# Sparse attention with a mixture of experts: where a part's third gather enters the list that orders the instructions

## The chip, the cores and the metric

The kernel runs on one core of a Trainium2 chip. The metric is the device time of one execution in microseconds (us), lower is better. Times of the kernel before are from three runs; the rows come from one more execution, taken with the profiler.

## What is computed

The input is a batch of 8 with 8 heads, 576 positions and a head width of 64. Half of the heads attend to the 32 positions behind each one, the other half to every 32nd position. The result, 4608 tokens by 512, goes through a gate that picks two of eight experts for each token, and each expert is a two-layer network of width 1024. All in float32:

```python
def _attn_ref(q, k, v):
    scores = np.matmul(q, k.transpose(0, 1, 3, 2)) / np.sqrt(D)
    mask_local = (rel >= 0) & (rel < 32)                      # heads 0 to 3
    mask_strided = (rel >= 0) & (pos[None, :] % 32 == pos[:, None] % 32)
    attn = softmax(np.where(masks, scores, -1e9))
    return np.matmul(attn, v)

def _moe_ref(x, w_gate, w_noise, noise, w1, w2):              # x: 4608 x 512
    noisy = x @ w_gate + np.log1p(np.exp(x @ w_noise)) * noise
    top2, top2_w = the two best experts of a token and their softmax weights
    for e in range(8):
        for k in range(2):
            mask = top2[:, k] == e
            out[mask] += top2_w[mask, k, None] * (np.maximum(x[mask] @ w1[e], 0.0) @ w2[e])
```

## The kernel before

**Two kinds of work in one stream.** The attention runs batch by batch and writes its rows to x_dram in the chip's memory. After the last unit of a batch a routing step (route) computes the gate, and its twelve indirect scatters on POOL (line 824, each behind a small memset on line 823) put an entry for each token and choice into the table tab, one list per expert: token number, weight, row of x. The expert work reads these lists. Parts of the first three experts' lists are fixed ahead of time so that their work can begin while the attention of later batches is still running; TensorE then has attention and expert work in turn, and the expert work fills what the attention leaves.

**A part (a job).** The lists are cut into parts of two or three blocks; a block is 128 rows, and a last one in a list can be a tail of 64. Each part goes through these steps:
- gather (line 908): SP loads the part's entries, POOL computes indices (lines 947, 950, 967, 969) and gathers the rows of x, block by block, into the tile xg. xg is a ring two deep: the third block takes the place of the first. An early part (one whose rows are known before the last batch, whole in the code) gathers a block with one indirect DMA (line 973 of the kernel before). A late part gathers a block with four of them, each of 128 rows of 128 columns, and a tail with two (line 959).
- transposes (line 981): each block is transposed, by TensorE into a bank of PSUM in an early part (line 998) and by DVE into the tile xr, one deep, in a late part (line 1002). ACT copies it rounded into xhi (line 1009) and DVE puts what the rounding left into xlo (line 1011). xhi and xlo are one deep, so a part's blocks can't be written before layer 1 of the part ahead is done with them.
- layer1 (line 1023): twelve matmuls for each of eight slices (line 1037), then ACT (line 1056) and DVE (line 1061).
- previous (line 1072): POOL gathers what the output holds so far for a block's tokens into prev (line 1077), a ring four deep.
- layer2 (line 1084): 24 matmuls for a whole block (line 1099), DVE multiplies by the weight and adds into prev (line 1124), and POOL scatters prev to the output (line 1129).

The loop over the parts makes, for part n in this order: two prev gathers of n, the gather step of n + 1, layer 1 of n, the transposes of n + 1, layer 2 of n. There are 32 parts counting the early ones; 16 of them have three blocks: two of the seven early parts, and 14 of the late ones, 8 of these with a tail as the third block.

**What sets the order.** Nothing above issues an instruction at once. Each step is a Piece (line 230) with an engine, a cost, a rank and the pieces that it waits for. issue_all (line 291) then runs a list schedule over all pieces with its own clock: on each engine it takes, among the pieces that could begin within 120 ns of the earliest, the one of lowest rank. A gather has the rank of its part's place (100 per part, plus 1), a prev gather plus 0 or 4, an output scatter plus 4 or more. The order that comes out is the order of each engine's queue on the chip. The chip's own waits are put in later, from what each instruction reads and writes, and an engine takes its queue in order: an instruction that waits holds up all behind it. On POOL that is every table scatter, every gather, every prev gather and every output scatter.

What a piece waits for in the list is fixed when it is made. For a place in a ring it is this, in the constructor:

```python
for s in self.alloc:
    r = s.ring
    if len(r.hist) >= r.k:
        self.deps += r.hist[-r.k].users
```

The users of a slot are the pieces that had named it by then. In the kernel before the gather step makes the gathers of all of a part's blocks before the transposes step makes the pieces that read them.

Of the kernel before, what the change touches and what calls it, by code (L numbers as in the profile page):

```python
# [22 lines left out]
def kernel(  # L23
# [12 lines left out]
    nc = tc.nc  # L36
# [43 lines left out]
    x_dram = dpool.tile([4 * NTOK, 128], F32, name="x_dram")  # L80
# [196 lines left out]
    def dma(fn, nbytes, rank, eng="SP", **kw):  # L277
        return Piece(eng, 690 if eng == "SP" else GAP, fn, rank, lat=nbytes, **kw)
# [137 lines left out]
    R = {}  # L416
# [485 lines left out]
    def experts(zero):  # L902
        W = {}
        known_stores = {n: [x for b in range(n) for x in stores[b]] for n in range(1, B + 1)}
        known_tab = {n: [x for b in range(n) for x in scatters[b]] for n in range(1, B + 1)}
        G_, XH, HT = {}, {}, {}

        def gather(n, rank):
            e, (start, nb, tail, hb) = jobs[n]
            known = hb * S  # L910

            whole = hb < B
            tb, gi = R["tabt"].new(), R["gix"].new()
            tx, gx = (None, None) if whole else (R["tabx"].new(), R["gxx"].new())

            def entries(dst, p0, n, how, bytes_, dims):
                def load(o):
                    ld = nc.sync.dma_start(dst(), dram(tab, (e * REG + p0) * 3, dims))
                    if hb < B:
                        for x, b in all_scatters:  # L920
                            if b >= hb:
                                tc.declare_no_dep(ld.ins, x.ins, reason=BEHIND)
                            else:
                                tc.add_manual_dep(ld.ins, x.ins.name, mybir.DependencyInfo(
                                    mybir.DependencyClass.Sync, mybir.DependencyReason.DATA), reason="entries of the list")
                        early_loads.append((ld, hb))
                dma(load, bytes_, rank if hb == B else 20 * NP * (hb - 1) + 10 * NP, after=known_tab[hb], expert=True,
                    far=4000, **how)

            if not whole:  # L930
                entries(lambda: tx.t[:, :4 * nb, :].rearrange("p b c -> p (b c)"), start, 128 * nb, {"alloc": [tx]}, 16384,
                        [[0, 4], [12 * nb, 32], [1, 12 * nb]])
            ng = tail // 32
            if tail:
                tx2 = R["tabx"].new()
                for g in range(ng):
                    entries(lambda g=g: tx2.t[:, g, :], start + 128 * nb + 32 * g, 32,
                            {"write" if g else "alloc": [tx2]}, 4096, [[0, 4], [3, 32], [1, 3]])
            entries(lambda: tb.t[:, :nb, :].rearrange("p b c -> p (b c)"), start, 128 * nb, {"alloc": [tb]}, 8192,
                    [[3 * nb, 4], [12 * nb, 32], [1, 3 * nb]])  # L940
            if tail:
                entries(lambda: tb.t[:tail, nb, :], start + 128 * nb, tail, {"write": [tb]}, 4096,
                        [[3, tail], [1, 3]])
            rows_known = 4 * known - 4

            def xindices(o):
                nc.gpsimd.tensor_scalar(gx.t[:, :nb, :], tx.t[:, :4 * nb, 2].rearrange(
                    "p (g b) -> p b g", g=4), float(rows_known), qoff[:, 0:1], op0=ALU.min, op1=ALU.add)
                if tail:
                    nc.gpsimd.tensor_scalar(gx.t[:, nb, :ng], tx2.t[:, :ng, 2], float(rows_known),  # L950
                                            qoff[:, 0:1], op0=ALU.min, op1=ALU.add)
            if not whole:
                Piece("POOL", 360 if tail else 230, xindices, rank, read=[tx] + ([tx2] if tail else []), alloc=[gx],
                      expert=True)
            xs = []
            for i in () if whole else range(nb + (tail > 0)):
                xg = R["xg"].new()
                for g in range(4 if i < nb else tail // 32):
                    dma(lambda o, i=i, g=g, xg=xg: nc.gpsimd.indirect_dma_start(  # L959
                        out=xg.t[:, g, :], out_offset=None, in_=x_dram[:4 * known, :],  # L960
                        in_offset=bass.IndirectOffsetOnAxis(ap=gx.t[:, i, g:g + 1], axis=0)),
                        65536, rank, eng="POOL", read=[gx], after=known_stores[hb], expert=True,
                        **({"write": [xg]} if g else {"alloc": [xg]}))
                xs.append(xg)

            def indices(o):
                nc.gpsimd.tensor_scalar(gi.t[:, :nb], tb.t[:, :nb, 0], known - 1, None, op0=ALU.min)
                if tail:
                    nc.gpsimd.tensor_scalar(gi.t[:tail, nb:nb + 1], tb.t[:tail, nb, 0:1], known - 1, None, op0=ALU.min)
            Piece("POOL", 300 if tail else 170, indices, rank, read=[tb], alloc=[gi], expert=True)  # L970
            for i in range(nb) if whole else ():
                xg = R["xg"].new()
                dma(lambda o, i=i, xg=xg: nc.gpsimd.indirect_dma_start(  # L973
                    out=xg.t.rearrange("p g c -> p (g c)"), out_offset=None,
                    in_=x_dram.rearrange("(t q) c -> t (q c)", q=4)[:known, :],
                    in_offset=bass.IndirectOffsetOnAxis(ap=gi.t[:, i:i + 1], axis=0)),
                    262144, rank, eng="POOL", read=[gi], after=known_stores[hb], expert=True, alloc=[xg])
                xs.append(xg)
            G_[n] = (tb, gi, xs)

        def transposes(n, rank):

# [2 lines left out]
            xh, xl = R["xhi"].new(), R["xlo"].new()  # L985
            XH[n] = (xh, xl)
            for i in range(nb + (tail > 0)):
                xg = G_[n][2][i]
                rows = 128 if i < nb else tail
                ng = rows // 32  # L990
                cols = slice(128 * i, 128 * i + rows)
# [15 lines left out]
                def view(xr=xr, rows=rows):  # L1007
# [3 lines left out]
                Piece("DVE", dve(4 * rows), lambda o, view=view, cols=cols: nc.vector.tensor_tensor(  # L1011
                    xl.t[:, :, cols], view(), xh.t[:, :, cols].bitcast(F32), ALU.subtract),
                      rank, read=[xr, xh], expert=True, **{how: [xl]})

        counts = {}

# [131 lines left out]
        for n, (e, (start, nb, tail, hb)) in enumerate(jobs):  # L1148
            nb += tail > 0
            others = [x for y in range(E) if y != e for x in out_done[y]]  # L1150
            rank = ER + 100 * n
# [29 lines left out]
    for c in range(NTOK // ZC):  # L1181
        zero.append(dma(
            lambda o, c=c: nc.sync.dma_start(out[ZC * c:ZC * c + ZC, :].rearrange("(p c) (a d) -> p (c a) d", p=128, a=4),
                                             zeros[:, None, :].to_broadcast([128, 4 * ZC // 128, 128])), 786432,
# [3 lines left out]
    for u in range(NU):  # L1188
        rank = 10 * u
# [20 lines left out]
    with tc.If(longest > CAP):  # L1210
        with ExitStack() as octx:
# [4 lines left out]
            for e in range(E):  # L1216
                left = nc.values_load(over[:1, e:e + 1], engines=ENG, min_val=0, max_val=NTOK - CAP)
                with tc.If(left > 0):
                    nc.sync.dma_start(w1t, dram(w1, e * DM * FF, [[FF, 128], [128 * FF, ND], [1, FF]]))
                    nc.sync.dma_start(w2t, dram(w2, e * DM * FF, [[DM, 128], [128 * DM, NF], [1, DM]]))  # L1220
                    with tc.For_i(0, left, 128) as it:
                        tb = ow.tile([128, 3], I32, name="tb")
                        nc.sync.dma_start(tb, tab[bass.ds(it + (e * REG + CAP), 128), :])
                        gi = ow.tile([128, 1], I32, name="gi")
                        nc.vector.tensor_scalar(gi, tb[:, :1], NTOK - 1, None, op0=ALU.min)
                        gx = ow.tile([128, 4], I32, name="gx")
                        xg = ow.tile([128, 4, 128], F32, name="oxg")
                        for c in range(4):
# [3 lines left out]
                                                         in_offset=bass.IndirectOffsetOnAxis(ap=gx[:, c:c + 1], axis=0))  # L1232
# [49 lines left out]
```

## Time and profile before

| what | us |
|---|---|
| median of three runs | 1108.83 |
| lowest and highest of them | 1102.39, 1113.18 |
| the profiled execution, its own time | 1104.51 |
| its span, first to last instruction | 1102.80 |
| TensorE busy in the span | 1064.4 |
| POOL busy in the span | 553.8 |
| DVE busy in the span | 607.6 |

The profiled execution is one run, 4.3 us under the median. Its own time is 1.71 us more than its span. PE is TensorE, DVE is VectorE, ACT is ScalarE, POOL is GpSimd and SP the engine that issues plain DMAs. Matmuls overlap each other, so a matmul's own duration is longer than its share of the time; the busy times count an overlap once. The granted clock (PEclk) is the mean over a stretch of what TensorE was given: 1.00 is 2.4 GHz and 0.50 is 1.2 GHz.

### The profile page before, as it was taken

The page shows a single profiled execution, that of the slowest core. Times are in us where ns is not written, and L with a number is a line of the kernel's source. Part 1 is how long each engine was busy: PE and PEld are TensorE (multiplying, and loading weights), DVE is VectorE, ACT ScalarE, POOL GpSimd, SP SyncE. Part 2 cuts the span into 40 slices and gives each one's busy share as a digit, 9 for nine tenths or more (in the row PEclk, how much of TensorE's full clock was granted, in tenths as well). Part 3 has the DMA queues.
Part 4 walks back from the last instruction along what each step waited for, and adds up shares of the span by engine and source line. Part 5 has one row for each costly group of instructions (what it writes and reads, how often), then busy time and mean ns, then how long its engine had stood idle before and what let it go on. Part 6 is the DMA issues. An engine that isn't in the chain of part 4 may idle for free.

```text
span 1102.8 us, 23359 instructions
## 1 busy us (share of the span) xinstructions
PE 1064.4 (97%) x8645; PEld 938.3 (85%) x8645; DVE 607.6 (55%) x1606; ACT 432.8 (39%) x1131; POOL 553.8 (50%) x734
## 2 busy tenths in 40 slices
PE   8898899999799999999999999999999999999995
PEld 7677678889688989898998989898988898898994
DVE  7789976776465223655673456345534553474341
ACT  6689975677353212423341224113312331142120
POOL 1045543510763455656676555655656464657530
PEclk8999999999899999999999999999999999999998
DMA  8999998887534332455554236223622452253210
GB/s 173 230 212 230 240 237 228 218 238 199 144 103 138 91 104 77 135 148 149 156 168 141 71 101 189 79 70 106 185 81 64 121 166 76 69 158 97 72 59 23
DMA packets 169482, 152.93 MB, mean 139 GB/s; under 512 B 52651, under 2 KB 137131, under 8 KB 169348
## 3 DMA queue, kind: packets, MB, share of 16 engines
q1 hardware_dynamic: 145028, 92.30, 33.4%
q0 software_dynamic: 24320, 58.87, 17.7%
q8 instruction: 82, 1.34, 0.5%
q14 instruction: 52, 0.43, 0.1%
HBM read 112.76 MB, written 39.39 MB: 138 GB/s over the span
## 4 chain that ended last, share of the span: by engine, by line
PE 82%; DVE 5%; issue 5%; DMA 4%; ACT 3%; POOL 0%; POOLq 0%; DVEq 0%; SPq 0%
PE bankE L1099 5%; PE bankF L1099 5%; PE bankG L1099 5%; PE bankC L1099 5%; PE bankG L1037 5%; PE bankF L1037 5%; PE bankA L1099 5%; PE bankH L1037 5%; PE bankC L1037 5%; PE bankA L1037 5%; PE bankD L1099 4%; PE bankB L1037 4%; PE bankD L1037 4%; PE bankE L1037 4%; PE bankH L1099 4%
## 5 line engine op out<-in xcount | busy, mean ns | idle before, releaser
L959 POOL DMA_INDIRECT xg<-x_dram,gxx x240 | 241.4, 1006 | 105.1 <-issue 55.7
L1129 POOL DMA_INDIRECT out_dram<-prev,tabt x80 | 82.1, 1026 | 103.7 <-DVE prev L1124 45.9
L1077 POOL DMA_INDIRECT prev<-out_dram,gix x80 | 77.3, 966 | 92.1 <-issue 39.5
L824 POOL DMA_INDIRECT tab<-ent,addr x96 | 92.2, 960 | 57.9 <-issue 15.6
L1002 DVE STREAM_TRANSPOSE xr<-xg 128x512 f32<-128x512 f32 (+1 forms) x64 | 66.3, 1037 | 12.7 <-DMA xg<-x_dram,gxx 11.2
L1009 ACT CAST xhi<-xr 128x512 fp32r<-128x512 f32 (+1 forms) x64 | 37.8, 591 | 69.9 <-DVE xr L1002 69.9
L894 ACT CAST w2hi<-wraw 128x512 fp32r<-128x512 f32 x80 | 47.4, 619 | 29.2 <-PE bankA L1108 7.4
L895 DVE TENSOR_TENSOR w1lo<-wraw,w1hi 128x512 fp32r<-128x512 f32 x80 | 54.7, 686 | 3.5 <-ACT w1hi L894 1.0
L895 DVE TENSOR_TENSOR w2lo<-wraw,w2hi 128x512 fp32r<-128x512 f32 x80 | 52.7, 684 | 3.5 <-ACT w2hi L894 2.2
L1011 DVE TENSOR_TENSOR xlo<-xr,xhi 128x512 fp32r<-128x512 f32 (+1 forms) x64 | 42.1, 658 | 18.4 <-ACT xhi L1009 17.2
L894 ACT CAST w1hi<-wraw 128x512 fp32r<-128x512 f32 x80 | 49.0, 614 | 1.4 <-DMA wraw<-in_moe_w_dram 1.2
L973 POOL DMA_INDIRECT xg<-x_dram,gix x16 | 16.8, 1050 | 58.4 <-PE bankD L998 42.8
L1056 ACT ACTIVATE hhi<-bankG 128x256 fp32r<-128x256 f32 (+2 forms) x34 | 14.3, 421 | 70.9 <-PE bankG L1037 70.9
L1037 PE MATMUL bankG<-xhi,w1hi 128*128 128x256 f32 (+3 forms) x136 | 41.2, 303 | 0.0
L1037 PE MATMUL bankG<-xhi,w1lo 128*128 128x256 f32 (+3 forms) x136 | 40.3, 296 | 0.0
L1037 PE MATMUL bankG<-xlo,w1hi 128*128 128x256 f32 (+3 forms) x136 | 40.1, 295 | 0.0
L1037 PE MATMUL bankF<-xhi,w1hi 128*128 128x256 f32 (+3 forms) x132 | 39.9, 302 | 0.0
L1037 PE MATMUL bankH<-xhi,w1hi 128*128 128x256 f32 (+3 forms) x132 | 39.7, 301 | 0.0
L1037 PE MATMUL bankA<-xhi,w1hi 128*128 128x256 f32 (+3 forms) x132 | 39.6, 300 | 0.0
L1037 PE MATMUL bankC<-xhi,w1hi 128*128 128x256 f32 (+3 forms) x132 | 39.6, 300 | 0.0
L1037 PE MATMUL bankF<-xhi,w1lo 128*128 128x256 f32 (+3 forms) x132 | 39.4, 298 | 0.0
L1037 PE MATMUL bankF<-xlo,w1hi 128*128 128x256 f32 (+3 forms) x132 | 39.3, 298 | 0.0
(666 smaller groups left out, 3573.1 us busy)
## 6 DMA issues: line engine op xcount, KB each, us to landing
wraw<-in_moe_w_dram SPq DMA_DIRECT2D x160, 256.0 KB
out_dram<-zeros SPq DMA_DIRECT2D x12, 768.0 KB
ks<-in_k_dram SPq DMA_DIRECT2D x15, 320.0 KB
qs<-in_q_dram SPq DMA_DIRECT2D x15, 320.0 KB
vraw<-in_v_dram SPq DMA_DIRECT2D x30, 160.0 KB
raw<-in_k_dram SPq DMA_DIRECT2D x16, 288.0 KB
v_l<-in_v_dram SPq DMA_DIRECT2D x16, 288.0 KB
raw<-in_q_dram SPq DMA_DIRECT2D x16, 288.0 KB
```

What stands on the lines that cost most here:

```text
L824: st = nc.gpsimd.indirect_dma_start(out=tab, out_offset=bass.IndirectOffsetOnAxis(ap=s["addr"].t[:, t, kk:kk + 1], axis=0), in_=s["ent"].t ...
L894: Piece("ACT", act(512) + 30, lambda o: nc.scalar.copy(hi.t, raw.t), rank, read=[raw], alloc=[hi], expert=True)
L895: Piece("DVE", dve(512), lambda o: nc.vector.tensor_tensor(lo.t, raw.t, hi.t.bitcast(F32), ALU.subtract), rank, read=[raw, hi], alloc=[lo] ...
L959: dma(lambda o, i=i, g=g, xg=xg: nc.gpsimd.indirect_dma_start(out=xg.t[:, g, :], out_offset=None, in_=x_dram[:4 * known, :], in_offset=bas ...
L973: dma(lambda o, i=i, xg=xg: nc.gpsimd.indirect_dma_start(out=xg.t.rearrange("p g c -> p (g c)"), out_offset=None, in_=x_dram.rearrange("(t ...
L1002: Piece("DVE", 8 * rows, lambda o, xg=xg, xr=xr, ng=ng, rows=rows: nc.vector.transpose(xr.t.rearrange("p (c x) -> p c x", c=ND)[:, :, :row ...
L1009: Piece("ACT", act(4 * rows), lambda o, view=view, cols=cols: nc.scalar.copy(xh.t[:, :, cols], view()), rank, read=[xr], expert=True, **{h ...
L1011: Piece("DVE", dve(4 * rows), lambda o, view=view, cols=cols: nc.vector.tensor_tensor(xl.t[:, :, cols], view(), xh.t[:, :, cols].bitcast(F ...
L1037: nc.tensor.matmul(ps.t[:, :width], a.t[:, 128 * d:128 * d + 128], c.t[:, d, :width], start=(m == 0), stop=(m == len(todo) - 1))
L1077: dma(lambda o: nc.gpsimd.indirect_dma_start(out=pv.t[:rows, :], out_offset=None, in_=out[:known, :], in_offset=bass.IndirectOffsetOnAxis( ...
L1099: nc.tensor.matmul(ps.t, HT[n, f][p[0]].t[:, cols], W2[n][f][p[1]].t, start=(m == 0), stop=(m == len(todo) - 1))
L1129: st = nc.gpsimd.indirect_dma_start(out=out[:known, :], out_offset=bass.IndirectOffsetOnAxis(ap=tb.t[:rows, i, 0:1], axis=0), in_=pv.t[:ro ...
```

## The change

The gather step makes only the gathers of a part's first two blocks and keeps a function, rows_of, that makes one block's gathers. The transposes step calls it for block i + 2 behind the pieces of block i. Ranks, costs, tiles and the work itself stay as they are.

```diff
--- before.py
+++ after.py
@@ -952,31 +952,33 @@
             if not whole:
                 Piece("POOL", 360 if tail else 230, xindices, rank, read=[tx] + ([tx2] if tail else []), alloc=[gx],
                       expert=True)
-            xs = []
-            for i in () if whole else range(nb + (tail > 0)):
+
+            def rows_of(i):
                 xg = R["xg"].new()
+                if whole:
+                    dma(lambda o: nc.gpsimd.indirect_dma_start(
+                        out=xg.t.rearrange("p g c -> p (g c)"), out_offset=None,
+                        in_=x_dram.rearrange("(t q) c -> t (q c)", q=4)[:known, :],
+                        in_offset=bass.IndirectOffsetOnAxis(ap=gi.t[:, i:i + 1], axis=0)),
+                        262144, rank, eng="POOL", read=[gi], after=known_stores[hb], expert=True, alloc=[xg])
+                    return xg
                 for g in range(4 if i < nb else tail // 32):
-                    dma(lambda o, i=i, g=g, xg=xg: nc.gpsimd.indirect_dma_start(
+                    dma(lambda o, g=g: nc.gpsimd.indirect_dma_start(
                         out=xg.t[:, g, :], out_offset=None, in_=x_dram[:4 * known, :],
                         in_offset=bass.IndirectOffsetOnAxis(ap=gx.t[:, i, g:g + 1], axis=0)),
                         65536, rank, eng="POOL", read=[gx], after=known_stores[hb], expert=True,
                         **({"write": [xg]} if g else {"alloc": [xg]}))
-                xs.append(xg)
+                return xg
+            xs = [] if whole else [rows_of(i) for i in range(2)]
 
             def indices(o):
                 nc.gpsimd.tensor_scalar(gi.t[:, :nb], tb.t[:, :nb, 0], known - 1, None, op0=ALU.min)
                 if tail:
                     nc.gpsimd.tensor_scalar(gi.t[:tail, nb:nb + 1], tb.t[:tail, nb, 0:1], known - 1, None, op0=ALU.min)
             Piece("POOL", 300 if tail else 170, indices, rank, read=[tb], alloc=[gi], expert=True)
-            for i in range(nb) if whole else ():
-                xg = R["xg"].new()
-                dma(lambda o, i=i, xg=xg: nc.gpsimd.indirect_dma_start(
-                    out=xg.t.rearrange("p g c -> p (g c)"), out_offset=None,
-                    in_=x_dram.rearrange("(t q) c -> t (q c)", q=4)[:known, :],
-                    in_offset=bass.IndirectOffsetOnAxis(ap=gi.t[:, i:i + 1], axis=0)),
-                    262144, rank, eng="POOL", read=[gi], after=known_stores[hb], expert=True, alloc=[xg])
-                xs.append(xg)
-            G_[n] = (tb, gi, xs)
+            if whole:
+                xs = [rows_of(i) for i in range(2)]
+            G_[n] = (tb, gi, xs, rows_of)
 
         def transposes(n, rank):
 
@@ -985,7 +987,8 @@
             xh, xl = R["xhi"].new(), R["xlo"].new()
             XH[n] = (xh, xl)
             for i in range(nb + (tail > 0)):
-                xg = G_[n][2][i]
+                xs, rows_of = G_[n][2:]
+                xg = xs[i]
                 rows = 128 if i < nb else tail
                 ng = rows // 32
                 cols = slice(128 * i, 128 * i + rows)
@@ -1011,6 +1014,9 @@
                 Piece("DVE", dve(4 * rows), lambda o, view=view, cols=cols: nc.vector.tensor_tensor(
                     xl.t[:, :, cols], view(), xh.t[:, :, cols].bitcast(F32), ALU.subtract),
                       rank, read=[xr, xh], expert=True, **{how: [xl]})
+                if i + 2 < nb + (tail > 0):
+
+                    xs.append(rows_of(i + 2))
 
         counts = {}
```

## Rows read from the trace of the kernel before

**Rows 1.** The page: the span, and each engine's busy time.
```profile
span 1102.8 us, 23359 instructions
...
PE 1064.4 (97%) x8645; PEld 938.3 (85%) x8645; DVE 607.6 (55%) x1606; ACT 432.8 (39%) x1131; POOL 553.8 (50%) x734
```

**Rows 2.** Stretches: length; busy PE, PEld, DVE, ACT, POOL; PEclk, DMA share, GB/s.
```profile
0.00:168.00 168.00, 148.09 (x2336) 119.46 (x2337) 137.29 (x554) 132.13 (x419) 62.39 (x140) 0.95 0.97 218
168.00:252.00 84.00, 83.99 (x1058) 72.84 (x1058) 59.44 (x220) 56.58 (x170) 27.06 (x46) 1.00 0.92 236
252.00:276.00 24.00, 24.00 (x345) 22.02 (x344) 16.85 (x54) 17.37 (x49) 0.00 (x0) 1.00 0.67 182
276.00:282.00 6.00, 3.71 (x27) 3.23 (x26) 3.46 (x24) 2.53 (x8) 4.50 (x9) 1.00 0.86 188
282.00:288.00 6.00, 6.00 (x43) 4.98 (x43) 2.92 (x15) 2.31 (x5) 4.90 (x11) 0.72 0.67 176
288.00:297.00 9.00, 9.00 (x105) 7.38 (x105) 4.85 (x18) 4.82 (x17) 5.60 (x9) 1.00 0.35 96
297.00:302.00 5.00, 1.32 (x31) 0.92 (x29) 1.09 (x3) 0.26 (x1) 3.68 (x4) 0.87 0.40 113
302.00:308.00 6.00, 6.00 (x69) 4.57 (x61) 2.95 (x10) 2.29 (x10) 4.87 (x14) 0.54 0.30 85
308.00:364.00 56.00, 55.75 (x419) 49.16 (x420) 33.68 (x104) 23.64 (x55) 27.24 (x47) 1.00 0.49 133
364.00:1060.00 696.00, 696.00 (x4065) 627.52 (x4064) 336.60 (x594) 187.51 (x393) 407.67 (x454) 1.00 0.38 114
1060.00:1102.80 42.80, 30.54 (x179) 26.26 (x178) 8.50 (x15) 3.33 (x9) 5.91 (x6) 0.88 0.10 32
```

**Rows 3.** Waits, 225 to 312 us: who waited for whom, total, times, longest.
```profile
POOL xg L973 <- PE bankD L998: 41.6, 1, 41.6
...
DVE prev L1124 <- DMA prev<-out_dram,gix: 6.8, 1, 6.8
...
PE bankF L550 <- DVE prev L1124: 3.7, 1, 3.7
...
PE bankC L998 <- DMA xg<-x_dram,gix: 2.3, 1, 2.3
```

**Rows 4.** POOL in order of time: start, duration, instruction, idle before it.
```profile
234.79 0.20 POOL L812 COPY ent<-wt 96x12 f32<-96x12 f32 x1 [0.80 <-DVE wt L806]
276.63 0.97 POOL L973 DMA_INDIRECT xg<-x_dram,gix  x1 [41.65 <-PE bankD L998]
...
277.91 0.93 POOL L824 DMA_INDIRECT tab<-ent,addr  x1 [0.21 <-POOL spacer L823]
...
291.33 0.91 POOL L824 DMA_INDIRECT tab<-ent,addr  x1 [0.21 <-issue]
...
293.86 1.01 POOL L1129 DMA_INDIRECT out_dram<-prev,tabt  x1 [0.30 <-DVE kT_s L286]
297.41 1.00 POOL L1077 DMA_INDIRECT prev<-out_dram,gix  x1 [2.54 <-DMA out_dram<-prev,tabt]
```

**Rows 5.** The chain that ended last, 270 to 312 us: start, duration, what.
```profile
276.63 4.71 DMA xg<-x_dram,gix
...
303.93 2.86 PE bankA L1099 x6
...
307.98 1.59 PE bankA L1099 x6
```

**Rows 6.** Waits of the whole span, POOL for the DVE transposes.
```profile
POOL xg L959 <- DVE xr L1002: 19.3, 15, 3.2
```

**Rows 7.** POOL, DVE and the chain around a late part's layer 1.
```profile
558.37 0.94 POOL L959 DMA_INDIRECT xg<-x_dram,gxx  x1 [0.30 <-DVE w1lo L895]
...
564.22 0.69 DVE L1011 TENSOR_TENSOR xlo<-xr,xhi 128x512 fp32r<-128x512 f32 x1
...
568.25 2.08 PE bankG L1037 x12
```

## The prediction

> **What bounds the kernel now.** I read the page's busy line first: TensorE is busy 1064.4 of 1102.8 us [rows 1], so the whole kernel can win at most the 38.4 us in which it stands still, plus what a low clock costs. Next I read the stages, in the table of stretches [rows 2], for where those 38.4 us lie. The reader is to see that they lie in three places. 19.9 us (168.00 - 148.09) are in the first 168 us, before the expert work is under way. 12.3 us (42.80 - 30.54) are in the tail after the last matmul. From 168 to 276 and from 364 to 1060 TensorE has no gap at all (0.01 us), and 0.25 us are left in 308 to 364. What remains are two short holes: 2.29 us in 276 to 282 and 3.68 us in 297 to 302. After each of them the granted clock is low (0.72 in 282 to 288, 0.54 in 302 to 308), where all other stretches from 168 to 1060 show 1.00.
>
> Then I read who ended those holes. The list of waits from 225 to 312 us [rows 3] names them: 2.3 us of a transpose (line 998) for a gather xg, and 3.7 us of the score matmuls (line 550) for the DVE step that adds a block into prev (line 1124); that DVE step itself had stood 6.8 us before the gather of prev. Above both stands a POOL wait of 41.6 us, of xg on line 973 for the transposes.
>
> Last I read POOL in order of time [rows 4]. At 234.79 us it copies the entries of a batch, and then it does nothing until 276.63, when the third gather of the part with three blocks goes out. Behind it, back to back, come twelve scatters into the table (277.91 to 291.33), two output scatters (to 293.86) and the prev gathers (from 297.41). So both holes have one cause. The gather was put in POOL's queue some 40 us before the transposes that free its place in the two-deep ring xg; POOL takes its queue in order, so all of that was late.
>
> **The change part by part.** *The place in the list.* A ring's third allocation waits for the users of the first, as far as they are known when it is made (the constructor of Piece). Before, all three gathers of a part are made ahead of the transposes, so the list knows of the first two gathers only and lets the third go as soon as the first has landed; the real wait is then POOL's. After, the third gather is made behind block 0's transposes, cast and subtraction, so the list itself holds it back. Up to 234.79 us nothing differs in the list's inputs, so the start (19.9 us) stays, and so does the tail.
>
> *What is moved.* Sixteen parts have three blocks: two of them early parts with one gather each (line 973). Of the fourteen late parts, counted by the code, eight end in a 64-row tail (two gathers) and six have a whole third block (four gathers). That is 2 + 16 + 24 = 42 of 256 gathers. None is added or removed, the bytes are the same, and SP's queue issues nothing for them. Each is moved back past what POOL has ready: table scatters, output scatters, prev gathers. No wait is added: the wait for the transposes is the one POOL already had.
>
> *The early part at 235 us.* What comes free is POOL from 235 to 276 (0.00 us busy in 252 to 276 [rows 2]). The queued work takes about 16.2 us from 277.6 to 293.9, and a few us more for the prev gathers [rows 4]; it fits in those 41 us, beside TensorE work which is full there. The gather itself still leaves at about 276.6 and lands 4.7 us later [rows 5], but the list now knows this and can put other TensorE work (the layer-2 matmuls of the part before, 1.6 us per six [rows 5]) ahead of the third transpose, where before TensorE stood for it. Terms:
> - the hole for xg: -2.29 us [rows 2, 3];
> - the hole for prev: -3.68 us [rows 2, 3];
> - the low clock behind them. From the granted clock it is 0.28 x 6 = 1.68 us in 282 to 288, 0.46 x 6 = 2.76 us in 302 to 308, and at most 0.2 us in 297 to 302, 4.6 together. From the instructions it is a little less: six layer-2 matmuls take 2.86 us at the low clock and 1.59 us at the full one [rows 5], a factor of 1.8 and not 2. The busy time at 1.2 GHz is 4.6/0.5 = 9.2 us, which at 1.8 costs 4.1. I take the middle, -4.3 us.
>
> That is -10.3 us. *What is given back:* with the holes gone, another wait can be next, an attention step on ACT or DVE. The nearest rows are 0.25 us of 56 in the stretch behind and 0.01 of 84 in the one before; the farthest is the start, 19.9 of 168, which in the 32 us from 276 to 308 would be 3.8 us. I take 0.3, as the neighbours have it, and keep 0 to 3.8 for the range.
>
> *The other early part and the fourteen late ones.* From 308 to 364 TensorE loses 0.25 us, and from 364 to 1060 nothing. POOL waits 19.3 us in 15 places for the DVE transposes there [rows 6], but no TensorE wait hangs on them, so their going brings nothing: 0 us. Can moving the gathers cost? In the part with 384 columns the last gather of the third block is issued at 558.37, its low half is done at 564.22 + 0.69 = 564.91, and layer 1 begins at 568.25 [rows 7]: 3.3 us to spare. A gather or scatter issue takes about 1.3 us with its gap, so two of them ahead of the third block (2.6 us) cost nothing and three (3.9 us) would cost 0.6. The gather's rank comes before output scatters', and a block's place comes free before the second block's gathers have all gone, so I take 0, with 0 to +22 us as bounds (below).
>
> *One rule against the change.* In the 84 us from 168 to 252 POOL was busy 27.06 us and DVE 59.44, and TensorE still 83.99 [rows 2]: side by side they cost TensorE nothing. The Trainium skill (SBUF — State Buffer, its part on the engines' ports and the DMA ports) says that GpSimd and VectorE share a pair of ports under an exclusive lock, whose loser stands for the whole instruction. By that rule POOL work that moves beside a busy DVE would slow DVE; the rows of 168 to 252 don't bear it out in TensorE's time, so the sum takes 0 for it, and what it would do at the worst is rival 4.
>
> *Sum.* 1104.51 us is the profiled execution (span 1102.80); less 10.0 it is 1094.5. The median of the runs shown, 1108.83, is 4.3 us above that execution, so I forecast **1099 us**, 0.9% below it. One per cent, 11 us, is about what a measurement of this kernel can tell from no change; the forecast lies just inside.
>
> **The rivals.**
> 1. *Only the first hole goes.* Prev stays late through another link: its gather also waits for the output scatters' landing, and the DVE step for its turn. Then 2.29 + 1.68 = 4 us: 1105. For it: two links lie between POOL and TensorE [rows 3]. Against it: all of them start 40 us sooner.
> 2. *The third gathers come too late in the late parts (slower).* Place: the third block's transposes ahead of layer 1. It decides once more than two POOL issues are put before the third gather, that is over 3.3 us late. Price: a hole of about 2 us and the clock behind it 1.7, as at 276 us, 3.7 each. In the six parts with four gathers that is 22 us: 1121. Against it: the room above, and POOL is busy only 407.67 of 696 us [rows 2].
> 3. *The change doesn't do what it says.* The list's clock for the transposes runs ahead of the chip's, so POOL still stands at the third gather: 1108.
> 4. *POOL's moved work holds DVE.* Some 16 us of POOL work [rows 4] move from where DVE is light (4.85 of 9 us) to where it is busy (16.85 of 24, so 7.15 us free [rows 2]). If DVE stood through all of it, it would be 16 - 7.15 = 9 us late, and the gain would shrink to 1 us: 1108. Against it: 168 to 252 us, as said.
>
> **How the numbers follow.** Forecast 0.72 (1092 to 1105 by itself: the give-back of 3.8 us, and what the runs scatter). Rival 1: 0.12; rival 2: 0.07; rival 3: 0.05; rival 4: 0.04. The range 1090 to 1110 holds the forecast, rivals 1, 3 and 4, and leaves out rival 2 and the edges. Faster by over 1% (under 1097.7) takes a bit under half of the forecast's own case, 0.35. Slower by over 1% is rival 2 in part, 0.06. Within 1% is the rest, 0.59.
>
> **What would show it.** Right: POOL without the 41.6 us wait on line 973 and busy between 235 and 276 us; table scatters of that batch done before the third gather; no TensorE wait on prev; granted clock 1.00 from 168 us to the tail; TensorE's busy time lower by about 4 us and its idle time by 6; after 364 us the same picture shifted 10 us earlier. Wrong: a TensorE wait on xg or xlo in the late stage, a new low-clock stretch, or POOL still standing at a third gather.

## The result and the profile after

| | us |
|---|---|
| kernel before, median of 15 runs (lowest, highest) | 1108.05 (1102.39, 1113.18) |
| changed kernel, median of 15 runs (lowest, highest) | 1098.10 (1095.13, 1101.51) |
| ratio, 95% interval | 0.9913, 0.9899 to 0.9927 |
| profiled execution of the changed kernel, its own time and its span | 1098.46, 1096.70 |

The changed kernel is 9.95 us (0.9%) faster, and the interval is clear of no change. The forecast was 1099 us, 0.9 us above the median that was measured.

The page of the changed kernel, the lines that answer to [rows 1]:

```profile
span 1096.7 us, 23359 instructions
...
PE 1062.7 (97%) x8645; PEld 939.4 (86%) x8645; DVE 607.4 (55%) x1605; ACT 432.4 (39%) x1132; POOL 552.5 (50%) x734
```

There are the same number of instructions and of matmuls, 1.7 us less of TensorE's busy time, and 6.1 us less of span. Where these went is read from the stretches, which answer to [rows 2] with the same columns:

```profile
0.00:168.00 168.00, 147.33 (x2278) 119.70 (x2280) 134.52 (x541) 130.38 (x413) 58.91 (x135) 0.91 0.94 212
168.00:252.00 84.00, 83.99 (x1087) 73.34 (x1088) 60.22 (x225) 54.93 (x163) 34.59 (x61) 1.00 0.89 228
252.00:276.00 24.00, 23.06 (x308) 21.18 (x307) 17.15 (x54) 17.57 (x54) 11.94 (x18) 1.00 0.88 231
276.00:282.00 6.00, 6.00 (x73) 5.15 (x72) 2.06 (x7) 3.16 (x10) 1.91 (x3) 1.00 0.95 268
282.00:288.00 6.00, 6.00 (x56) 5.01 (x55) 4.74 (x31) 3.92 (x12) 1.20 (x3) 1.00 1.09 331
...
297.00:302.00 5.00, 5.00 (x91) 3.72 (x90) 1.74 (x5) 2.04 (x10) 2.93 (x6) 1.00 0.02 1
302.00:308.00 6.00, 6.00 (x53) 5.29 (x51) 2.47 (x9) 2.48 (x8) 3.06 (x7) 1.00 0.20 53
308.00:364.00 56.00, 56.00 (x407) 50.38 (x407) 32.76 (x99) 23.41 (x54) 24.15 (x41) 1.00 0.47 129
364.00:1054.00 690.00, 690.00 (x4031) 621.73 (x4030) 335.30 (x591) 186.03 (x390) 403.59 (x448) 1.00 0.39 115
```

The reader is to see three things. TensorE has no gap from 276 to 1054 us, and the granted clock is 1.00 all through it: both holes and both falls of the clock are gone. POOL has 11.94 us of work in 252 to 276, where it had none. And 0.94 us (24.00 - 23.06) are missing in that stretch, where nothing was missing before.

The waits answer to [rows 3]. TensorE's only wait between 168 and 1090 us is the first line; POOL's waits for a place are the other two (one of the window 225 to 312, one of the whole span, which answers to [rows 6]):

```profile
PE bankE L509 <- DMA ks<-in_k_dram: 0.9, 1, 0.9
```

```profile
POOL xg L959 <- PE bankG L1001: 3.8, 1, 3.8
```

```profile
POOL xg L966 <- DVE xr L1005: 20.6, 17, 3.2
```

The 41.6 us have become 3.8. The late parts' waits for the DVE transposes (line 1005, line 1002 before) have not gone: 20.6 us in 17 places against 19.3 in 15. I come back to that. POOL in order of time, answering to [rows 4]:

```profile
238.93 0.20 POOL L812 COPY ent<-wt 96x12 f32<-96x12 f32 x1 [0.79 <-DVE wt L806]
...
243.87 0.95 POOL L824 DMA_INDIRECT tab<-ent,addr  x1 [4.73 <-issue]
...
263.14 0.91 POOL L824 DMA_INDIRECT tab<-ent,addr  x1 [0.22 <-issue]
265.19 1.01 POOL L1135 DMA_INDIRECT out_dram<-prev,tabt  x1 [1.14 <-ACT hhi L1062]
...
273.36 1.00 POOL L1083 DMA_INDIRECT prev<-out_dram,gix  x1 [5.36 <-DVE kT_l L286]
...
281.92 0.94 POOL L959 DMA_INDIRECT xg<-x_dram,gix  x1 [3.78 <-PE bankG L1001]
```

The scatters, the output scatters and the prev gathers now stand ahead of the third gather. **How much that is worth** is best read between two events that both traces have: from the third gather's issue to the first matmuls of layer 1 of its part. In the trace of before the latter is this line of the chain that ended last:

```profile
310.88 2.09 PE bankD L1037 x12
```

and in the changed kernel, with the line numbers moved by six:

```profile
305.13 2.09 PE bankA L1043 x12
```

Before, it took 310.88 - 276.63 = 34.25 us; after, 305.13 - 281.92 = 23.21 us: 11.04 us saved. The 0.94 us of the new wait for ks fall ahead of the third gather. From an event ahead of everything that the change moves, the copy of a batch's entries, to the same layer 1 it is 310.88 - 234.79 = 76.09 us before and 305.13 - 238.93 = 66.20 us after: **9.9 us saved**, the new wait included. The copy itself came 4.1 us later in this execution than before. Another execution of the same changed kernel (e11, below) has it at 235.61, only 0.8 us later, so the 4.1 us are a difference between executions and not the change's.

### The profile page after: what moved, and what is told of

Its sections match the earlier page's. It is cut to its first block, busy times and chain, and to the rows that moved or that the text cites. A ratio compares the mean times of both kernels' runs of the same rounds, so it can differ in the third digit from the quotient of the medians.

```text
span 1096.7 us, 23359 instructions
## 1 busy us (share of the span) xinstructions
PE 1062.7 (97%) x8645; PEld 939.4 (86%) x8645; DVE 607.4 (55%) x1605; ACT 432.4 (39%) x1132; POOL 552.5 (50%) x734
## 3 DMA queue, kind: packets, MB, share of 16 engines
q0 software_dynamic: 24320, 58.87, 17.6%
## 4 chain that ended last, share of the span: by engine, by line
PE 90%; DMA 3%; DVE 3%; ACT 2%; issue 1%; POOL 0%; POOLq 0%; DVEq 0%
PE bankF L1105 6%; PE bankC L1105 5%; PE bankG L1043 5%; PE bankD L1105 5%; PE bankH L1043 5%; PE bankC L1043 5%; PE bankA L1043 5%; PE bankE L1043 5%; PE bankB L1043 5%; PE bankG L1105 5%; PE bankH L1105 5%; PE bankF L1043 5%; PE bankE L1105 5%; PE bankD L1043 4%; PE bankA L1105 4%; PE bankB L1105 4%
## 5 line engine op out<-in xcount | busy, mean ns | idle before, releaser
L1062 ACT ACTIVATE hhi<-bankH 128x256 fp32r<-128x256 f32 (+2 forms) x33 | 14.0, 423 | 70.3 <-PE bankH L1043 70.3
L1043 PE MATMUL bankA<-xhi,w1lo 128*128 128x256 f32 (+3 forms) x132 | 39.2, 297 | 0.0
L1043 PE MATMUL bankC<-xhi,w1lo 128*128 128x256 f32 (+3 forms) x132 | 39.2, 297 | 0.0
```

Source lines behind the costliest of these rows:

```text
L1043: nc.tensor.matmul(ps.t[:, :width], a.t[:, 128 * d:128 * d + 128], c.t[:, d, :width], start=(m == 0), stop=(m == len(todo) - 1))
L1062: Piece("ACT", act(width) + 30, lambda o: nc.scalar.activation(hh.t[:, :width], ps.t[:, :width], AF.Relu), rank, read=[ps], alloc=[hh], ex ...
```

## The experiments

Twelve runs, in four series, each series on one chip with the kernel before run beside it. The chip of the first series was slower for every kernel (the kernel before: 1155.02 us, against 1106 to 1108 on the others), so its ratios are not compared with the others' (each ratio is to the kernel before on the same chip, with its 95% interval in brackets), and its four questions were asked again (e8, e9, e10, e12).

**Ahead of them: the order of the queues.** The lists of instructions of each engine, in the order in which the schedule puts them, tell what the edit moves. On POOL two gathers move, both of early parts: the third of part 3 (counted from 0) goes from ahead of a batch's twelve scatters to behind these, two output scatters and four prev gathers; the third of part 4 changes places with one index computation. With the edit in the early parts alone, the queues of all five engines are those of the changed kernel; with the edit in the late parts alone, they are those of the kernel before. So the late parts' forty gathers stay where they were, and the experiments ask which of the two moved gathers matters, and through what.

TensorE's own order changes too. In part 3 the third transposes stood 3.6 us of other work behind the first ones before (275.61 to 281.48, less the wait of 2.29); in the changed kernel (e11) they stand 9.04 us behind (276.54 to 285.58). So there are two candidates for the gain, POOL's freed queue and TensorE's new order, and e9 and e10 below have one of them each.

### One gather moved alone (e1, e8; e2, e12)

```diff
-            xs = [] if whole else [rows_of(i) for i in range(2)]
+            xs = [] if whole else [rows_of(i) for i in range(nb + (tail > 0))]
...
             if whole:
-                xs = [rows_of(i) for i in range(2)]
+                xs = [rows_of(i) for i in range(2 if n == 3 else nb)]
...
-                if i + 2 < nb + (tail > 0):
+                if i + 2 < nb + (tail > 0) and i + 2 >= len(xs):
```

This is the changed kernel with the deferral in part 3 only (late parts as before); with `n == 4` it is part 4 only.

> Only the third gather of the first early part with three blocks enters the list behind its transposes; the other early part and all late parts are as in the kernel before. Theory (the whole gain is the one POOL wait of 41.6 us at 235 us): ratio 0.991, as for the whole change, no TensorE wait on prev, granted clock 1.00 from 168 us to the tail. Rival (the late parts, where POOL waited 19.3 us for the DVE transposes, carry the gain): 1.000. Rival (the other early part has a share): 0.993 to 0.996.

> The deferral of early part 3 alone, the other parts as before. My theory (this one gather holds POOL's queue, and with it the scatters and the gathers of prev behind it): the whole gain, a ratio of 0.990 to 0.992, POOL's longest wait for a place gone, no fall of the clock between 282 and 308 us. Rival (both moved gathers are needed, half the gain each): 0.995 to 0.996.

> Only the third gather of the second early part with three blocks enters the list behind its transposes. Theory: ratio 1.000 within 0.2%, both holes of the kernel before still there (2.3 and 3.7 us), the 41.6 us POOL wait too. Rival (this part has a share): 0.995 to 0.997.

> The deferral of early part 4 alone, part 3 and the rest as before. My theory (that gather changes places with one index computation only and no table scatter stands behind it): 0.999 to 1.001, POOL's longest wait for a place still near 41.6 us and TensorE's two waits as before, 2.3 and 3.7 us. Rival (both moved gathers bring half the gain each): 0.995 to 0.996.

Part 3 alone (e8) takes 1099.04 us, a ratio of 0.9916 [0.9887, 0.9945]; on the first chip (e1) it is 0.9831 [0.9797, 0.9865]. Part 4 alone (e12) takes 1106.24 us, 1.0010 [0.9992, 1.0027]; on the first chip 0.9997 [0.9972, 1.0022]. With part 3 alone (e8) POOL's longest wait for the third gather and TensorE's only wait between 168 and 1040 us are these:

```profile
POOL xg L959 <- PE bankG L1001: 4.5, 1, 4.5
```

```profile
PE bankE L509 <- DMA ks<-in_k_dram: 0.4, 1, 0.4
```

The waits from 225 to 312 us with part 4 alone (e12) are those of before, with the second hole 1.6 us longer:

```profile
POOL xg L959 <- PE bankD L1001: 41.7, 1, 41.7
...
PE bankF L550 <- DVE prev L1130: 5.3, 1, 5.3
...
PE bankC L1001 <- DMA xg<-x_dram,gix: 2.3, 1, 2.3
```

The clock tells why it is longer. Behind the first hole, 2.30 us long as before, it didn't fall in this execution:

```profile
282.00:288.00 6.00, 6.00 (x79) 4.94 (x78) 4.66 (x16) 3.06 (x8) 4.91 (x11) 1.00 0.53 126
```

In the kernel before it was 0.72 in the same stretch [rows 2], which cost 1.68 us; here those were not lost, TensorE came to the second wait that much sooner, and waited 5.32 us in place of 3.68. From the third gather to layer 1 it still took 308.90 - 274.32 = 34.58 us. So the low clock behind the first hole came in one of two executions in which TensorE's order was the same up to there, and the one without it won nothing by that.

One of 256 gathers carries the whole gain, as far as the intervals tell (the whole change in the same series as e8, e11: 0.9897 [0.9874, 0.9921]). The one with twelve scatters, two output scatters and four prev gathers queued behind it counts; the one that changes places with an index computation doesn't.

### The order as before, the place no longer waited for (e3, e9)

```diff
-                xg = R["xg"].new()
+                xg = R["xg" if i < 2 else "xr"].new()
...
-                    out=xg.t.rearrange("p g c -> p (g c)"), out_offset=None,
+                    out=xg.t.rearrange("p g c -> p (g c)") if i < 2 else xg.t, out_offset=None,
...
```

This is the kernel before, with an early part's third block gathered into the tile xr, which only late parts use, and transposed from there. The gather stays ahead of the batch's scatters in POOL's queue, and there is no place that it waits for.

> The kernel before, but the third block of the two early parts goes into the tile xr, which stands empty until the late parts, so its gather needs no place that the transposes free. It stays where it was in the list, with the first two. Theory (what cost was POOL standing): ratio 0.990 to 0.992, third gather at about 235 us, no hole from 276 to 308 us. Rival (the gain is the list's better knowledge, which puts other TensorE work ahead of the third transposes): 0.995 or above, for the list knows no more here than before.

> The order of before, with a place of its own for the third block of an early part, so that no gather waits for a place. My theory (the wait for the place costs, not the order of the list): 0.990 to 0.992. Rival (the order of the gathers on POOL, which stays as before here, is what costs): 0.998 to 1.002.

E9 takes 1097.61 us, 0.9908 [0.9884, 0.9932]; on the first chip 0.9840 [0.9793, 0.9887]. POOL in order of time (e9):

```profile
234.94 1.05 POOL L973 DMA_INDIRECT xg<-x_dram,gix  x1 [1.03 <-DMA x_dram<-xo]
236.50 0.94 POOL L973 DMA_INDIRECT xr<-x_dram,gix  x1 [0.50 <-DVE nz L753]
```

and the third transposes on TensorE:

```profile
283.91 0.68 PE L999 MATMUL bankH<-ident,xr 128*128 128x128 f32 x4
```

The third gather leaves at 236.50 with the first two of its part, ahead of the twelve scatters as in the kernel before, and the gain is the same. So it does no harm by itself that it stands ahead of them; that it waits there does. TensorE's new order isn't needed for the gain either: the third transposes stand 3.4 us behind the first ones (at 280.49), as in the kernel before.

### The two holes, closed one at a time (e4, e10; e5)

The first edit closes the first hole and leaves POOL as it was: the schedule is told that the third transposes come 6 us behind the first ones, so that TensorE has other work ahead of them.

```diff
-                    Piece("PE", 108 * ND, tr, rank, read=[xg], psum=xr, expert=True)
+                    behind = [first] if i == 2 else []
+                    turn_it = Piece("PE", 108 * ND, tr, rank, read=[xg], after=behind, psum=xr, expert=True)
+                    if i == 0:
+                        first = turn_it
+                    if behind:
+                        turn_it.lag = 6000
```

In the schedule's clock a piece then begins its lag later than the pieces that it waits for.

> The kernel before, but the list lets the early parts' third transposes begin only 6 us behind the first ones, so TensorE does other work while the third gather lands; POOL's queue at 235 us stays as before, with its 41 us wait. Additive theory (my prediction's first rival: the first hole and its low clock go, the second stays): gain 2.3 + 1.7 = 4 us, ratio 0.9964, second hole 3.7 us. Rival theory (the second hole's end is set by POOL's chain from the third gather on, so TensorE that comes there sooner waits longer): ratio 0.999 to 1.001, the second hole grows from 3.7 to about 7 us.

> The order of before on POOL, with TensorE's wait for the gathered block put later in TensorE's list, so that the first hole is filled and POOL's stall stays. My theory (the second hole's end is set by POOL's own chain, some 25 us behind the third gather, so that it takes over what the first gives back): 0.998 to 1.001, and the wait for prev grows from 3.7 us to 6 or 7. Rival (the holes add up, and the first one is gone): 0.996 to 0.997, with the wait for prev at 3.7 us.

E10 takes 1105.22 us, 0.9985 [0.9967, 1.0003]; on the first chip 0.9977 [0.9946, 1.0007]. The stretches, POOL's lines and TensorE's in e10:

```profile
276.00:282.00 6.00, 6.00 (x69) 4.91 (x69) 2.28 (x7) 3.14 (x7) 1.29 (x3) 1.00 1.05 295
282.00:288.00 6.00, 6.00 (x62) 5.06 (x61) 5.51 (x39) 2.64 (x9) 4.90 (x11) 1.00 0.84 191
288.00:297.00 9.00, 9.00 (x109) 7.55 (x107) 5.66 (x24) 5.53 (x17) 7.36 (x14) 1.00 0.39 84
297.00:302.00 5.00, 0.69 (x9) 0.29 (x6) 0.00 (x0) 0.26 (x1) 2.15 (x3) 0.86 0.28 105
302.00:308.00 6.00, 2.53 (x44) 2.29 (x44) 2.70 (x7) 0.28 (x2) 4.64 (x10) 0.50 0.62 171
```

```profile
280.49 0.97 POOL L974 DMA_INDIRECT xg<-x_dram,gix  x1 [41.65 <-PE bankD L999]
...
301.25 1.00 POOL L1083 DMA_INDIRECT prev<-out_dram,gix  x1 [2.54 <-DMA out_dram<-prev,tabt]
```

```profile
305.47 0.40 PE L551 MATMUL bankF<-mask_s,twin 64*64 64x288 bf16 x1 [7.79 <-DVE prev L1130]
```

The first hole and the fall of the clock behind it are gone, 2.29 + 1.68 = 4.0 us, and the second hole has grown from 3.68 to 7.79, by 4.1. Its end stands at 305.47 - 280.49 = 24.98 us behind the third gather; in the kernel before, whose score matmuls begin with the line below, it was 301.65 - 276.63 = 25.02, and in e12 299.39 - 274.32 = 25.07.

```profile
301.65 0.39 PE L550 MATMUL bankF<-mask_s,twin 64*64 64x288 bf16 x1 [3.68 <-DVE prev L1124]
```

That distance is POOL's own chain: from the third gather to the first prev gather 20.76 us of scatters and of waiting for an output scatter to land, 3.4 for the prev gather's landing, 0.8 for the DVE step. In these three traces TensorE waits for its end, however early it comes.

This edit also gives TensorE the order of the changed kernel in part 3:

```profile
288.51 0.65 PE L999 MATMUL bankE<-ident,xg 128*128 128x128 f32 x4
```

The third transposes stand 9.04 us behind the first ones (at 279.47), as in e11. With POOL's stall left in place that order wins nothing clear of noise, and in e9 POOL without its stall wins the whole gain in the old order. So it is POOL's stall that cost.

The second edit fills both holes with matmuls of zeros, to keep the clock up: nine ahead of the third transposes and eighteen ahead of the score matmuls. They are extra work, in banks that the next matmuls start anew.

```diff
         def scores(o):
+            for _ in range(18 if u == 30 else 0):
+                nc.tensor.matmul(sc[0].t.rearrange("r (a x) -> r a x", a=2), warm[:, :128],
+                                 warm[:, None, :].to_broadcast([128, 2, 256]), start=True, stop=True)
...
+                        for _ in range(9 if (n, i) == (3, 2) else 0):
+                            nc.tensor.matmul(xr.t.rearrange("r (a x) -> r a x", a=2), warm[:, :128],
+                                             warm[:, None, :].to_broadcast([128, 2, 256]), start=True, stop=True)
```

> The kernel before with extra matmuls on a tile of zeros in TensorE's queue, just ahead of the two waits: 9 of 512 columns (1.9 us) ahead of the early part's third transposes, 18 (3.9 us) ahead of the score matmuls that wait for prev. They write a bank that is overwritten right behind. Theory (the low clock comes from the idle holes, and the second hole's end is set by POOL's chain): granted clock 1.00 from 276 to 308 us, the second wait longer by what the first clock fall cost, and only the second fall's 2.7 us are won: ratio 0.9976. Additive theory: 4.3 us, 0.9961. Rival (the clock falls for another reason): clock still near 0.5 behind the holes, ratio 1.000 or slower.

E5 takes 1106.07 us, 0.9995 [0.9978, 1.0012]: the expected 0.9976 was a miss. POOL's third gather, TensorE's filling and its wait, and the stretches from 300 us:

```profile
274.43 0.97 POOL L976 DMA_INDIRECT xg<-x_dram,gix  x1 [41.65 <-PE bankD L1004]
```

```profile
293.61 4.05 PE L542 MATMUL bankH<-zeros 128*128 128x512 bf16 x18
...
299.39 0.28 PE L553 MATMUL bankF<-mask_s,twin 64*64 64x288 bf16 x1 [1.46 <-DVE prev L1130]
```

```profile
300.00:302.00 2.00, 1.43 (x22) 0.97 (x13) 1.83 (x9) 0.00 (x0) 1.51 (x7) 0.93 0.67 209
302.00:304.00 2.00, 2.00 (x6) 1.16 (x4) 0.86 (x2) 1.49 (x8) 1.78 (x3) 0.50 0.08 16
```

The first fall is not there, and TensorE comes to the second wait sooner. But the hole's end is again at 299.39 - 274.43 = 24.96 us, the eighteen matmuls were over before that and left a wait of 1.46 us, and the clock fell to 0.50 behind it all the same. That the zeros kept the clock up behind the first hole is not shown: in e12 it stayed up there without them. From the third gather to layer 1 it took 308.36 - 274.43 = 33.9 us, against 34.25 before.

### A gather that really comes too late (e6), and the changed kernel again (e7, e11)

In e6 the changed kernel's late parts hold the third block's gathers until the second block's subtraction (line 1014) is done.

```diff
-                        65536, rank, eng="POOL", read=[gx], after=known_stores[hb], expert=True,
+                        65536, rank, eng="POOL", read=[gx], after=known_stores[hb] + list(behind), expert=True,
...
-                if i + 2 < nb + (tail > 0):
+                if i == (0 if hb < B else 1) and nb + (tail > 0) > 2:
...
-                    xs.append(rows_of(i + 2))
+                    xs.append(rows_of(2, [] if hb < B else [low]))
```

> The changed kernel, but in the fourteen late parts the third gather waits in the list for the second block's lower half (xlo) as well, so it is really late. Prices my rival that ends slower. From the rows before: the second block's lower half ended at 562.34 in the part with 384 columns; four issues of 1.26 us, 2 us to land, 2.4 us of transposing, rounding and subtracting give about 572, 3.7 us behind the start of layer 1; with 1.7 us of low clock 5.4 us for each of six parts, and about nothing for the eight with a tail: 1098 + 32 = 1130, ratio 1.02 to the kernel before. Rival (there is more room than I read): ratio 0.991 as without it.

> The changed kernel once more, on the chip of the two runs before it: ratio 0.991, interval 0.990 to 0.993; the start to 168 us within 3 us of that of the kernel before.

> The changed kernel beside the three above on one chip, as the measure of the whole gain: 0.990 to 0.992 by all theories.

E6 takes 1147.41 us, 1.0365 [1.0337, 1.0393], which is 50.3 us over the changed kernel beside it (e7: 1097.10, 0.9911 [0.9876, 0.9945]) and 17 us over the 1130 that I had expected. TensorE's waits of the whole span in e6, of which these are the longest:

```profile
PE bankH L1043 <- ACT xhi L1012: 8.4, 2, 6.2
PE bankB L1043 <- ACT xhi L1012: 5.9, 1, 5.9
PE bankC L1043 <- ACT xhi L1012: 4.7, 1, 4.7
PE bankF L1043 <- ACT xhi L1012: 4.1, 1, 4.1
PE bankG L1043 <- DVE xlo L1014: 3.1, 2, 2.0
```

Layer 1's waits for xhi and xlo are 32.1 us in 15 places; after 168 us the changed kernel has one of 0.3 us in e7 and none in its other two traces. The six parts with 384 columns hold 28 us of them, 2.1 to 6.6 us each; of the eight parts with a tail four wait 1.0 us each. The rest of the loss is a slower TensorE: it is busy 1080.0 us with the same 8645 matmuls for which e7 takes 1059.8, 20 us more, and the granted clock over 364 to 1000 us is 0.98 where e7 has 1.00.

In the third series the changed kernel (e11) took 1096.46 us, 0.9897 [0.9874, 0.9921]. Its profiled execution has no wait for ks, and is the cleaner mirror of before: the two lines below are POOL's third gather and the chain's first matmuls of layer 1.

```profile
277.56 0.94 POOL L959 DMA_INDIRECT xg<-x_dram,gix  x1 [4.64 <-PE bankG L1001]
```

```profile
300.77 2.09 PE bankA L1043 x12
```

The interval is 23.21 us again. Layer 1 begins 310.88 - 300.77 = 10.1 us earlier than before, and the span is 1102.8 - 1092.4 = 10.4 us shorter. From the copy of the batch's entries to layer 1 it is 300.77 - 235.61 = 65.16 us, 10.9 less than before.

## Why the prediction was right, point by point

**The cause** held. One gather, put in POOL's queue some 40 us ahead of the transposes that free its place, held everything behind it. Removing that wait by order (e8) or by another place (e9) gives the whole gain, as far as the intervals tell; leaving it (e10, e5, e12) gives none that is clear of noise.

**The sum** held: 10.0 us was forecast, 9.9 measured between matched events (10.9 in e11), and the medians of the result and of the two later series with the changed kernel differ by 9.95, 9.35 and 10.81. By its terms: the two holes went as sized, 2.29 and 3.68. For the low clock there are left 11.04 - 5.97 = 5.07 us, where I took 4.3 and the granted clock alone gave 4.6; that remainder can hold a few matmuls that the new order puts ahead of the gather, and the two weren't separated. The give-back was 0.94 us in one execution of the changed kernel and none in another (e11), against the 0.3 I took; what was late next was not ACT or DVE but a load of keys. So the low clock was taken some 0.8 us too small and, in the first execution, the give-back 0.6 us too small; that the sum came out so close is in part because these two cancel. The signs held too. TensorE's busy time was to fall by about 4 us and its idle time by 6: in e11 they fell by 3.8 and 6.6, in the first execution, which lost more in its first 168 us, by 1.7 and 4.4.

**The edit's reach was told wrong**, without effect on the sum. "42 of 256 gathers" and "each is moved back past what POOL has ready" describe what the code defers; in the queues two gathers move. In the late parts the schedule had put the third gathers no earlier before. So the 19.3 us of POOL's waits at DVE transposes did not go, as the step "their going brings nothing" supposed; they are there still, at 20.6, and cost nothing as before.

**Rival 1 had a wrong price.** It took the holes to be additive: with only the first one gone, 4 us. E10 is the nearest case, though what keeps prev late there is POOL's stall and not another link. Its profile gives the 4 us back within 30 us: the distance from the third gather to the second hole's end is set by POOL, so time won ahead of it is only waited for later. Its runs lie between a gain of 3.7 us and a loss of 0.3, so a gain of 4 us is just outside. My terms were a right sum but not separate gains: the second hole had to go for any of them to count. E12 shows the same of the first fall of the clock: it was absent there, and the way from the third gather to layer 1 was no shorter for it.

**Rival 2's mechanism is real, and it didn't happen.** In e6, which holds the gathers of all fourteen late parts with a third block, the six parts that I had counted do carry most of it, but the price was too low: I took a hole of 2 us and 1.7 us of low clock for each, 22 us in all, and e6 lost 4.7 us in waits for each of the six, 4 us in the tails, and 20 us of slower TensorE (52.8 us between the two spans, 50.3 between the medians). E6 holds the gathers until the second block is done, which is later than the rival had them, so it bounds that case and does not price it. The change puts none of these gathers later, so the price was never due.

**Rival 3**, that the list's clock runs ahead of the chip's: 3.8 us of waiting are left at the third gather (4.6 in e11), and TensorE waits for nothing of POOL's from 168 to 1090 us.

**Rival 4**, POOL's moved work holding DVE, did not show. In e11 DVE is busy 16.90 us for 53 instructions in 252 to 276 us with 11.43 us of POOL work beside it; before it was 16.85 us for 54 with none [rows 2]:

```profile
252.00:276.00 24.00, 24.00 (x345) 22.37 (x346) 16.90 (x53) 17.60 (x53) 11.43 (x15) 1.00 0.91 242
```

Two of the subtractions that make w2lo, with both inputs in SBUF, took 1.41 us in e11 (from 254.01) with POOL busy all through them, and 1.40 us before (from 253.09) with POOL idle. The Trainium skill (SBUF — State Buffer, its part on SBUF's two sides) says that the loser of the port pair shared by VectorE and GpSimd stands for a whole instruction. It says so of VectorE instructions in a two-port mode, and of those with two inputs in SBUF against a GpSimd instruction that reads SBUF, which is narrower than the rule as I took it. In these rows DVE doesn't lose. What is longer is POOL's own work: a scatter that began while w2lo was being made took 1.23 us in e11 (the line below) and in e9 (at 250.27), where most take 0.91. That this is the lock of the ports was not tested.

```profile
257.39 1.23 POOL L824 DMA_INDIRECT tab<-ent,addr  x1 [0.61 <-ACT w2hi L894]
```

## What to carry to other kernels

Read the longest wait of an engine that seems half idle, and then what is queued behind it: an instruction that waits for a place costs by what stands behind it, not by its wait (one wait of 41.6 us cost 10 us here, and 20 us of other waits cost nothing). In a list schedule, make a ring's next user after the readers of the place it takes, or the list sees no reason to hold it. When two holes lie in one chain, find what sets the end of the last one before summing: closing an earlier one alone won nothing here that could be measured.

## What I had not expected of the hardware

On the chip of the first series the same hole was far larger. With part 4 alone (e2), that is with part 3's gather as before, the stretch from 308 to 336 us and two of the waits there read:

```profile
308.00:336.00 28.00, 11.87 (x114) 8.99 (x114) 6.07 (x26) 4.06 (x12) 16.43 (x30) 0.70 0.37 104
```

```profile
ACT qT_l L284 <- remote: 20.7, 1, 20.7
DVE rs L627 <- remote: 18.2, 1, 18.2
```

TensorE stands 16.1 us, ACT and DVE stand too, and the releaser is one that the profile can't name ("remote"). These two waits lie beside POOL's burst of scatters, and go with it (in e1 other waits with that releaser are left, the longest 8.2 us): from 300 to 345 us TensorE is busy 43.93 us with part 3 moved (e1) and 26.29 us without (e2), 17.6 us, which is about the 17.75 us between the medians (1155.02 and 1137.27). Why these two engines stood there was not tried and stays open; on the other chips no wait on that releaser appears in any trace.

The clock fell to 0.50 in e5 behind a wait of only 1.46 us which followed 4 us of matmuls of zeros. Before, it fell behind waits of 2.29 and 3.68 us; in e12 it stayed at 1.00 behind a wait of 2.30 us. So the length of the wait alone doesn't tell whether the clock falls, and filling most of the second hole with zeros didn't prevent it here.
